# A third load-and-output buffer, an earlier x load and turn, and weight combinations at other places, in a gated scan with a leaky MLP

## Chip, core and metric

One core of a Trainium2 chip runs the whole program. The metric is device time in microseconds (us), from the kernel's start to its end. Engines are named as in the profile: PE multiplies matrices and PEld loads its weights, DVE is the vector engine, ACT the scalar engine, POOL the general one, SP issues most DMAs. A line number such as L203 is a line of the kernel before; in the changed file the same lines stand up to four further on.

## What is computed

```python
sig = 1.0 / (1.0 + np.exp(-f_logit))            # x, f_logit: 4 x 6080 x 256, float32
f = lower_bound + (1.0 - lower_bound) * sig
for t in range(S):
    h = f[:, t] * h + (1.0 - f[:, t]) * x[:, t]
    y[:, t] = h
a = y.reshape(24320, 256) @ w_in                # 256 x 2048
out = np.maximum(0.01 * a, a) @ w_out           # 2048 x 256
```

## The kernel before

The 24320 tokens are cut into 24 blocks, 23 of 1024 tokens and a last one of 768. The hidden width 2048 is cut into eight groups g of 2 x 128 columns. A **slot** is one group of one block, (j, g), and slots run in the order of `seq`. The order of the instructions on every engine is written out by hand: the code is under a manual schedule, and each engine does its list in the order in which the calls stand.

Every float32 operand of a matmul is split into a high and a low part (wi_h and wi_l, yh and yl, gh and gl, the two halves of wo), so a product takes three matmuls. In blocks from 1 on a slot (`slot`, L379) forms the first layer by a scheme with seven products M1 to M7 of block matrices instead of eight, so the stationary weights have seven forms per group: four that are loaded, and three, at places 2 and 4 to 6 of wi_h and wi_l, with combinations of them (`combine_w` adds and subtracts on DVE, `split_c` writes the high parts on ACT and the low parts on DVE). A slot has 21 matmuls for the products and 24 for the second layer (`second`, called at once for the last quarter and through `old` in the next slot for the other three): 45.

Within such a slot PE does M1 into PSUM bank a, M5 into c, M2 into b, M6 into a, the old quarters between M6, M7, M4 and M3, and then one quarter of its own. ACT copies bank a after M1 (L389), after M6 (L396) and after M7 (L401); M6 writes to bank a too, so it waits for the copy at L389. DVE adds bank b (L393), bank c with M5 (L402) and bank c with M3 (L420) to those copies; M5 of the next slot writes bank c, so it waits for L420. For each of the four quarters ACT makes the high part gh (L309) and the full activation (L314), and DVE the low part gl (L319). The last quarter's pair on ACT waits for L420 and stands just ahead of the next slot's L389.

The next block is prepared in the slots of the present one. `hooks` says at which point of which slot: the points of a slot are C (after M1), a0 (after M2), A (after M6), B (ahead of M4), a3 (ahead of M3) and E (the end). In slot 1 the gate's logits are turned (`tl`, two DVE transposes at L203), in slot 2 x is turned (`tx`, the same line), in slots 2 and 3 the gate is formed on ACT (`th` at L206 and `f` at L209), from slot 3 on come u (L212), the scans (L176), differences (L222) and the splits into yh and yl (L227, L230). Block 0 has its own way for all this (`first_slot`, `plain_slot`); its slots form eight products, and between them weights of the later groups are loaded raw, as the two 32-bit halves of each number, decoded on ACT, DVE and POOL (`scale_w`, `decode_w`) and split (`split_w`). Combinations begin in slot 6 of block 0, two slots ahead of block 1's use of group 0, so in block 1 the slots 0 to 5 form those of groups 2 to 7.

The pool `ld` has two buffers of 16 KB per partition. In each block from 1 on they are taken in turn by the output tile of the block before (`new_osb` at C of slot 0), by the logits of the next block (`load` at the same point) and by its x (`load` after the second evacuation in slot 0, L425). All these DMAs stand on SP's queue in that order, with the eight output stores (`evacuate`, L302) between the two loads. `raw` has three buffers of 4 KB of its own in the pool `dw`. `combine_w` puts its result under the tag r, which `scale_w` uses too, with one buffer.

```python
old(s, 1, 1)                                         # L398, after hook("A")
product(a, j, g, M7, False)
act(out=c22[:, :n], in_=a[:, :n], func=ACTF.Copy)    # L401
vtt(out=c22[:, :n], in0=c[:, :n], in1=c22[:, :n], op=ALU.add)   # L402
```

Of the kernel before, what the change touches and what calls it, by code (L numbers as in the profile page):

```python
# [8 lines left out]
F32 = mybir.dt.float32  # L9
F32R = mybir.dt.float32r  # L10
U32 = mybir.dt.uint32
# [13 lines left out]
def tile_gated_scan_then_leaky_mlp(  # L25
# [10 lines left out]
    B, S, D = x.shape  # L36
    NT = B * S
    DFF = w_in.shape[1]
    P = 128
    KC = D // P  # L40
    NG = DFF // P // 2
# [5 lines left out]
    NB = len(starts)  # L47
# [3 lines left out]
    ff = f_logit.rearrange("b s d -> (b s) d")  # L51

    const = ctx.enter_context(tc.tile_pool(name="const", bufs=1))
    ld_p = ctx.enter_context(tc.tile_pool(name="ld", bufs=2))
    xt_p = ctx.enter_context(tc.tile_pool(name="xt", bufs=1))
    cy_p = ctx.enter_context(tc.tile_pool(name="cy", bufs=2))
    ys_p = ctx.enter_context(tc.tile_pool(name="ys", bufs=2))
# [16 lines left out]


    raw_t = {}
    part_t = {}

    def load_w(kind, g):
        r = dw_p.tile([P, 2, 256, 2], U32, tag="raw", name="raw", bufs=3)  # L80
        if kind == "i":
            v = w_in.bitcast(U32).rearrange("(k p) (h g f) -> g h p k f", p=P, h=2, f=2 * P)
            rv = r.rearrange("p h (k f) t -> p h k (f t)", k=2)
            for h in range(2):
                nc.sync.dma_start(out=rv[:, h], in_=v[g, h])
        else:
            v = w_out.bitcast(U32).rearrange("(h g p) f -> g p h f", p=P, h=2)
            nc.sync.dma_start(out=r.rearrange("p h f t -> p h (f t)"), in_=v[g])
        raw_t[kind, g] = r
# [36 lines left out]

    def combine_w(g):
        w = dw_p.tile([P, 4, P], F32, tag="a", name="a")
        c = dw_p.tile([P, 4, P], F32, tag="r", name="r")
        vtt(out=w, in0=wi_h[:, g, 0:4].bitcast(F32), in1=wi_l[:, g, 0:4].bitcast(F32), op=ALU.add)  # L130
        vtt(out=c[:, 0], in0=w[:, 2], in1=w[:, 3], op=ALU.add)
        vtt(out=c[:, 2], in0=w[:, 0], in1=w[:, 2], op=ALU.subtract)
        vtt(out=c[:, 1], in0=c[:, 0], in1=w[:, 0], op=ALU.subtract)
        vtt(out=c[:, 3], in0=w[:, 1], in1=c[:, 1], op=ALU.subtract)
        part_t["c", g] = c
# [61 lines left out]
    def x_piece(j, piece):  # L197
# [35 lines left out]
    hooks = {  # L233
        (1, "A"): [("tl", 0), ("tl", 1)],
        (2, "a0"): [("th", 0)],
        (2, "A"): [("f", 0)],
        (2, "B"): [("tx", 0)],
        (2, "a3"): [("tx", 1)],
        (3, "a0"): [("th", 1)],
        (3, "A"): [("f", 1), ("u", 0), ("scan", (0, 0))],  # L240
        (4, "A"): [("u", 1), ("scan", (0, 1))],
# [137 lines left out]
    def slot(s, hook):  # L379
        j, g = seq[s]  # L380
        n = sizes[j] // 2
        done = g == 0 and j > 0
        a = ps_a.tile([P, HM], F32, tag="a", name="pa")
        b = ps_b.tile([P, HM], F32, tag="b", name="pb")
        c = ps_b.tile([P, HM], F32, tag="c", name="pc")
        product(a, j, g, M1, True)
        hook("C")
        c11 = new_c()
        act(out=c11[:, :n], in_=a[:, :n], func=ACTF.Copy)  # L389
        product(c, j, g, M5, True)  # L390
        product(b, j, g, M2, True)
        hook("a0")
        vtt(out=c11[:, :n], in0=b[:, :n], in1=c11[:, :n], op=ALU.add)  # L393
        product(a, j, g, M6, False)
        c12 = new_c()
        act(out=c12[:, :n], in_=a[:, :n], func=ACTF.Copy)  # L396
        hook("A")
        old(s, 1, 1)  # L398
        product(a, j, g, M7, False)
        c22 = new_c()  # L400
        act(out=c22[:, :n], in_=a[:, :n], func=ACTF.Copy)  # L401
        vtt(out=c22[:, :n], in0=c[:, :n], in1=c22[:, :n], op=ALU.add)  # L402
        leaky_high((j, g, 0, 0), c11)
        leaky((j, g, 0, 0), c11, c11)
        old(s, 1, 0)
        if done:
            evacuate(j - 1, 0)
        low((j, g, 0, 0), c11)
        hook("B")
        leaky_high((j, g, 1, 1), c22)  # L410
        leaky((j, g, 1, 1), c22, c22)
        low((j, g, 1, 1), c22)
        product(a, j, g, M4, False)
        c21 = new_c()
        leaky_high((j, g, 1, 0), a)
        leaky((j, g, 1, 0), c21, a)
        old(s, 0, 1)
        hook("a3")
        product(c, j, g, M3, False)
        vtt(out=c12[:, :n], in0=c[:, :n], in1=c12[:, :n], op=ALU.add)  # L420
        low((j, g, 1, 0), c21)
        if done:
            evacuate(j - 1, 1)
            if j + 1 < NB:
                load(j + 1, "x")  # L425
        leaky_high((j, g, 0, 1), c12)
        leaky((j, g, 0, 1), c12, c12)
        second(j, g, 0, 0)
        low((j, g, 0, 1), c12)
        hook("E")  # L430
# [119 lines left out]
    with tc.manual_schedule():  # L550
# [17 lines left out]
        for s in range(1, len(seq)):  # L568
            j, g = seq[s]

            def hook(at):
# [16 lines left out]
                if j > 0 and (g, at) == (0, "C"):  # L588
                    new_osb(j - 1)
                    if j + 1 < NB:  # L590
                        load(j + 1, "l")
                c = s + 2 - NG
                if 0 <= c < NG:
                    if at == ("D" if j == 0 else "B"):
                        combine_w(c)
                    elif at == "E":
                        split_c(c)
                if j > 0:
                    for p in hooks_own.get((g, at), ()):
                        x_piece(j, p)  # L600
                if j + 1 < NB:
                    for p in hooks.get((g, at), ()):
                        x_piece(j + 1, p)

            (plain_slot if j == 0 else slot)(s, hook)
        e = len(seq)
# [35 lines left out]
```

## Time and profile before

| what | value |
|---|---|
| median of 3 runs | 2017.22 us (2016.95 to 2017.23) |
| the profiled execution, its time | 2017.16 us |
| its span, first to last instruction | 2015.3 us |
| granted TensorE clock, mean | 0.998 |
| busy: PE, PEld, DVE, ACT, POOL | 99%, 81%, 70%, 69%, 1% of the span |
| DMA | 84.6 MB, 42 GB/s on the mean |

A row of the timeline gives when an instruction started and how long it took; in brackets stand the idle time of its engine just ahead of it and what ended that. The next instruction on an engine often starts before the time of the one before it is over, so distances from start to start are compared here: DVE adds of 512 columns last 0.69 us and start 0.60 us apart when nothing holds them. A matmul's time overlaps the next ones in the same way.

### The profile page before, as it was taken

The numbers are of one execution on the slowest core, as the hardware profiler recorded it, in microseconds if no ns is written. First come the engines' busy times: TensorE is split into PE (matmuls) and PEld (weight loads), VectorE is DVE, ScalarE is ACT, GpSimd is POOL, SyncE is SP. The second block draws the span as 40 slices with busy tenths as digits, with TensorE's granted clock in tenths as the row PEclk, the third lists the DMA queues.
The fourth block names the chain that finished last, engine by engine and source line by source line (L and its number), as shares of the span: only waits on it lengthen the run. The fifth ranks groups of instructions, "written<-read, shape, count | busy, mean of one in ns | idle before, by whom it ended". The sixth has DMA issues, their size and how long they took to land.

```text
span 2015.3 us, 23212 instructions
## 1 busy us (share of the span) xinstructions
PE 1988.0 (99%) x8718; PEld 1627.1 (81%) x8718; DVE 1417.0 (70%) x2003; ACT 1399.3 (69%) x2352; POOL 28.0 (1%) x25
## 2 busy tenths in 40 slices
PE   8999999999999999999999999999999999999998
PEld 6777888888888888888888888888888888888888
DVE  7978676767776776767667776676766767676664
ACT  6766667766777667776677667776677666776665
POOL 2200000000000000000000000000000000000000
PEclk9999999999999999999999999999999999999999
DMA  9460522505325054160450514505134052250211
GB/s 187 85 63 1 63 36 28 63 1 63 42 22 63 3 61 50 14 63 10 54 57 7 64 18 46 63 1 63 26 37 63 1 63 35 28 58 0 37 22 16
DMA packets 584448, 84.60 MB, mean 42 GB/s; under 512 B 574096, under 2 KB 582288, under 8 KB 584336
## 3 DMA queue, kind: packets, MB, share of 16 engines
q1 hardware_dynamic: 581184, 82.57, 33.8%
q8 instruction: 68, 1.11, 0.2%
q10 hardware_dynamic: 3152, 0.56, 0.2%
q14 instruction: 44, 0.36, 0.1%
HBM read 58.20 MB, written 24.90 MB: 41 GB/s over the span
## 4 chain that ended last, share of the span: by engine, by line
PE 90%; DVE 6%; ACT 3%; issue 1%; DMA 0%; POOL 0%; DVEq 0%; POOLq 0%; ACTq 0%
PE o L281 48%; PE pa L259 25%; PE pc L259 11%; PE pb L259 6%; DVE xT L203 3%; DVE gl L319 1%; ACT c L314 1%; ACT gh L309 1%; DVE c L420 1%; ACT c L389 1%; DMA lld<-in_f_logit_dram 0%; DVE xT L176 0%; ACT wi_h L140 0%; DVE wi_l L125 0%; DVE osb L296 0%
## 5 line engine op out<-in xcount | busy, mean ns | idle before, releaser
L281 PE MATMUL o<-gh,wo 128*128 128x512 f32 (+1 forms) x3072 | 822.1, 389 | 0.0
L319 DVE TENSOR_TENSOR gl<-c,gh 128x512 fp32r<-128x512 f32 (+1 forms) x768 | 524.4, 686 | 270.5 <-ACT c L314 270.5
L281 PEld LDWEIGHTS o<-gh,wo 128*128 128x128 f32 x3072 | 575.5, 188 | 121.0
L309 ACT ACTIVATE gh<-c 128x512 fp32r<-128x512 f32 (+1 forms) x552 | 342.3, 620 | 193.8 <-DVE c L420 193.8
L281 PE MATMUL o<-gl,wo 128*128 128x512 f32 (+1 forms) x1536 | 472.3, 388 | 0.0
L314 ACT ACTIVATE c<-c 128x512 f32<-128x512 f32 (+1 forms) x552 | 346.5, 628 | 17.6
L281 PEld LDWEIGHTS o<-gl,wo 128*128 128x128 f32 x1536 | 288.0, 188 | 60.6
L259 PE MATMUL pa<-yh,wi_l 128*128 128x512 f32 (+1 forms) x768 | 303.2, 395 | 9.7 <-ACT c L389 5.5
L259 PE MATMUL pa<-yh,wi_h 128*128 128x512 f32 (+1 forms) x768 | 299.1, 389 | 0.9 <-ACT wi_h L123 0.9
L259 PE MATMUL pa<-yl,wi_h 128*128 128x512 f32 (+1 forms) x768 | 298.2, 388 | 0.1
L401 ACT ACTIVATE c<-pa 128x512 f32<-128x512 f32 (+1 forms) x184 | 109.0, 593 | 185.0 <-PE pa L259 182.1
L402 DVE TENSOR_TENSOR c<-pc,c 128x512 f32<-128x512 f32 (+1 forms) x184 | 126.0, 685 | 158.6 <-ACT c L401 154.4
L396 ACT ACTIVATE c<-pa 128x512 f32<-128x512 f32 (+1 forms) x184 | 109.1, 593 | 172.5 <-PE pa L259 169.9
L259 PEld LDWEIGHTS pa<-yh,wi_l 128*128 128x128 f32 x768 | 144.2, 188 | 52.0 <-ACT c L389 17.3
L393 DVE TENSOR_TENSOR c<-pb,c 128x512 f32<-128x512 f32 (+1 forms) x184 | 125.6, 683 | 77.6 <-PE pb L259 64.5
L420 DVE TENSOR_TENSOR c<-pc,c 128x512 f32<-128x512 f32 (+1 forms) x184 | 125.2, 680 | 64.3 <-PE pc L259 63.6
L259 PEld LDWEIGHTS pa<-yl,wi_h 128*128 128x128 f32 x768 | 144.2, 188 | 32.2 <-DVE yl L230 0.8
L259 PEld LDWEIGHTS pa<-yh,wi_h 128*128 128x128 f32 x768 | 144.3, 188 | 29.1 <-ACT wi_h L123 1.1
L259 PE MATMUL pc<-yh,wi_l 128*128 128x512 f32 (+1 forms) x384 | 152.5, 397 | 1.5 <-DVE c L420 1.5
L259 PE MATMUL pc<-yh,wi_h 128*128 128x512 f32 (+1 forms) x384 | 149.7, 390 | 0.0
L259 PE MATMUL pc<-yl,wi_h 128*128 128x512 f32 (+1 forms) x384 | 149.2, 389 | 0.0
L309 ACT ACTIVATE gh<-pa 128x512 fp32r<-128x512 f32 (+1 forms) x200 | 115.3, 576 | 7.0 <-PE pa L259 6.2
(76 smaller groups left out, 1675.9 us busy)
## 6 DMA issues: line engine op xcount, KB each, us to landing
lld<-in_f_logit_dram SPq DMA_DIRECT2D x92, 256.0 KB, 6.5
out_dram<-osb SPq DMA_DIRECT2D x184, 128.0 KB, 3.2
xld<-in_x_dram SPq DMA_DIRECT2D x91, 256.0 KB, 5.8
raw<-in_moe_w_in_dram SPq DMA_DIRECT2D x16, 256.0 KB, 3.5
raw<-in_moe_w_out_dram SPq DMA_DIRECT2D x8, 512.0 KB, 4.4
lld<-in_f_logit_dram SPq DMA_DIRECT2D x4, 192.0 KB, 5.8
xld<-in_x_dram SPq DMA_DIRECT2D x4, 192.0 KB, 5.0
out_dram<-osb SPq DMA_DIRECT2D x5, 96.0 KB, 4.2
```

The lines of the kernel that those rows point to most:

```text
L203: nc.vector.transpose(out=xs[j, nm][:, k], in_=loaded[j, nm][:, k].rearrange("p t d -> p (t d)"))
L259: nc.tensor.matmul(out=bank[:, :n], lhsT=a[:, g, w, :], rhs=b[:, i, :n], start=start and e == 0, stop=stop and e == 2, skip_group_check=True,)
L281: nc.tensor.matmul(out=o[k][:, :n], lhsT=wo[:, g, h, w, k * P:(k + 1) * P], rhs=v[:, :n], start=first and s == 0, stop=last and s == 2, sk ...
L309: act(out=gh[:, :n], in_=src[:, :n], func=ACTF.Prelu, alpha=0.01)
L314: act(out=dst[:, :n], in_=src[:, :n], func=ACTF.Prelu, alpha=0.01)
L319: vtt(out=gl[:, :n], in0=c[:, :n], in1=gh[:, :n].bitcast(F32), op=ALU.subtract)
L389: act(out=c11[:, :n], in_=a[:, :n], func=ACTF.Copy)
L393: vtt(out=c11[:, :n], in0=b[:, :n], in1=c11[:, :n], op=ALU.add)
L396: act(out=c12[:, :n], in_=a[:, :n], func=ACTF.Copy)
L401: act(out=c22[:, :n], in_=a[:, :n], func=ACTF.Copy)
L402: vtt(out=c22[:, :n], in0=c[:, :n], in1=c22[:, :n], op=ALU.add)
L420: vtt(out=c12[:, :n], in0=c[:, :n], in1=c12[:, :n], op=ALU.add)
```

## The change

The pool `ld` gets a third buffer, and its space is found by putting two of the three raw weight buffers of block 0 into a tile of that pool, which is given up afterwards. x of the next block is loaded at C of slot 0, straight after the logits, and turned as a pair at A of slot 2. The combinations of block 1 are formed at C instead of B, into the tag w (two buffers) instead of r; their split stands at A of the next slot, behind the other work of that point, instead of E of the same slot. In block 0 the combinations stay at D and E.

```diff
-    ld_p = ctx.enter_context(tc.tile_pool(name="ld", bufs=2))
+    ld_p = ctx.enter_context(tc.tile_pool(name="ld", bufs=3))
...
     raw_t = {}
+    raws = []
     part_t = {}
 
     def load_w(kind, g):
-        r = dw_p.tile([P, 2, 256, 2], U32, tag="raw", name="raw", bufs=3)
+        if not raws:
+            pair = ld_p.tile([P, 2, 2, 256, 2], U32, tag="ld", name="rawld")
+            raws.extend((dw_p.tile([P, 2, 256, 2], U32, tag="raw", name="raw"), pair[:, 0], pair[:, 1]))
+        r = raws[len(raw_t) % 3]
...
     def combine_w(g):
         w = dw_p.tile([P, 4, P], F32, tag="a", name="a")
-        c = dw_p.tile([P, 4, P], F32, tag="r", name="r")
+        c = dw_p.tile([P, 4, P], F32, tag="w", name="c", bufs=2)
...
-        (2, "A"): [("f", 0)],
-        (2, "B"): [("tx", 0)],
-        (2, "a3"): [("tx", 1)],
+        (2, "A"): [("f", 0), ("tx", 0), ("tx", 1)],
...
             evacuate(j - 1, 1)
-            if j + 1 < NB:
-                load(j + 1, "x")
...
                     if j + 1 < NB:
                         load(j + 1, "l")
+                        load(j + 1, "x")
                 c = s + 2 - NG
-                if 0 <= c < NG:
-                    if at == ("D" if j == 0 else "B"):
-                        combine_w(c)
-                    elif at == "E":
-                        split_c(c)
+                if 0 <= c < NG and at == ("D" if j == 0 else "C"):
+                    combine_w(c)
...
                     for p in hooks.get((g, at), ()):
                         x_piece(j + 1, p)
+                if 0 <= c < NG and j == 0 and at == "E":
+                    split_c(c)
+                elif 0 < c <= NG and at == "A" and ("c", c - 1) in part_t:
+                    split_c(c - 1)
```

Where the instructions stand is shown below at three places, before and after; the line numbers are those of either file, and PE's order is the same in both.

DVE in slot 2 of block 2 (every later block has the same rows): L393, L402 and L420 are the three adds of a slot, L319 the low parts, L203 the turns. Before:

```order
L393 TENSOR_TENSOR c<-pb,c 128x512
L402 TENSOR_TENSOR c<-pc,c 128x512
L319 TENSOR_TENSOR gl<-c,gh 128x512
L203 STREAM_TRANSPOSE xT<-xld 128x1024
L319 TENSOR_TENSOR gl<-c,gh 128x512
L203 STREAM_TRANSPOSE xT<-xld 128x1024
L420 TENSOR_TENSOR c<-pc,c 128x512
L319 TENSOR_TENSOR gl<-c,gh 128x512 x2
```

With the change (L395, L404, L422, L321 and L207 are the same lines, moved):

```order
L395 TENSOR_TENSOR c<-pb,c 128x512
L207 STREAM_TRANSPOSE xT<-xld 128x1024 x2
L404 TENSOR_TENSOR c<-pc,c 128x512
L321 TENSOR_TENSOR gl<-c,gh 128x512 x2
L422 TENSOR_TENSOR c<-pc,c 128x512
L321 TENSOR_TENSOR gl<-c,gh 128x512 x2
```

The two turns went from among the low parts, ahead of the third add, to between the first and the second add.

DVE in block 1, from the second add of slot 3 to the end of that slot. Before:

```order
L402 TENSOR_TENSOR c<-pc,c 128x512
L319 TENSOR_TENSOR gl<-c,gh 128x512
L130 TENSOR_TENSOR a<-wi_h,wi_l 128x512
L131 TENSOR_TENSOR r<-a 128x128
L132 TENSOR_TENSOR r<-a 128x128
L133 TENSOR_TENSOR r<-r,a 128x128
L134 TENSOR_TENSOR r<-a,r 128x128
L319 TENSOR_TENSOR gl<-c,gh 128x512
L420 TENSOR_TENSOR c<-pc,c 128x512
L319 TENSOR_TENSOR gl<-c,gh 128x512 x2
L141 TENSOR_TENSOR wi_l<-r,wi_h 128x128
L141 TENSOR_TENSOR wi_l<-r,wi_h 128x384
```

With the change, from the last low parts of slot 3 to the split in slot 4, which is followed by the second add:

```order
L321 TENSOR_TENSOR gl<-c,gh 128x512 x2
L134 TENSOR_TENSOR a<-wi_h,wi_l 128x512
L135 TENSOR_TENSOR c<-a 128x128
L136 TENSOR_TENSOR c<-a 128x128
L137 TENSOR_TENSOR c<-c,a 128x128
L138 TENSOR_TENSOR c<-a,c 128x128
L395 TENSOR_TENSOR c<-pb,c 128x512
L216 SCALAR_TENSOR_TENSOR xT<-lT,xT 128x1024
L180 SCALAR_TENSOR_TENSOR xT<-lT,xT 128x512
L186 COPY cy<-xT 128x1
L145 TENSOR_TENSOR wi_l<-c,wi_h 128x128
L145 TENSOR_TENSOR wi_l<-c,wi_h 128x384
```

The five instructions of a combination went to ahead of the first add, and the two of the split to ahead of the second; on ACT the split's two instructions went from ahead of L389 to ahead of L401.

SP's queue at the end of block 0 and in block 1. Before:

```order
L85 DMA raw<-in_moe_w_in_dram 128x2x256 x2
L88 DMA raw<-in_moe_w_out_dram 128x2x512
L152 DMA lld<-in_f_logit_dram 32x64x32 x4
L302 DMA out_dram<-osb 64x16x32 x8
L152 DMA xld<-in_x_dram 32x64x32 x4
```

With the change:

```order
L89 DMA rawld<-in_moe_w_in_dram 128x2x256 x2
L92 DMA raw<-in_moe_w_out_dram 128x2x512
L156 DMA lld<-in_f_logit_dram 32x64x32 x4
L156 DMA xld<-in_x_dram 32x64x32 x4
L304 DMA out_dram<-osb 64x16x32 x8
```

The four loads of x now stand ahead of the eight stores of the block before instead of behind them.

## Rows read from the trace of the kernel before

**Rows 1.** The page's part 1: busy us (share of the span) xinstructions.

```profile
PE 1988.0 (99%) x8718; PEld 1627.1 (81%) x8718; DVE 1417.0 (70%) x2003; ACT 1399.3 (69%) x2352; POOL 28.0 (1%) x25
```

**Rows 2.** PE's timeline: start us, us, instruction [idle before <-releaser]; blocks 0, 1, 12, 21.

```profile
52.45 0.50 PE L259 MATMUL pa<-yh,wi_l 128*128 128x512 f32 x1 [0.76 <-DVE wi_l L125]
...
110.82 0.39 PE L259 MATMUL pa<-yh,wi_l 128*128 128x512 f32 x1
...
189.46 0.39 PE L259 MATMUL pa<-yh,wi_l 128*128 128x512 f32 x1
...
1009.16 0.39 PE L259 MATMUL pa<-yh,wi_l 128*128 128x512 f32 x1
...
1019.46 0.39 PE L259 MATMUL pa<-yh,wi_l 128*128 128x512 f32 x1
...
1061.14 0.51 PE L259 MATMUL pa<-yh,wi_l 128*128 128x512 f32 x1 [0.15 <-ACT c L389]
...
1808.13 0.51 PE L259 MATMUL pa<-yh,wi_l 128*128 128x512 f32 x1 [0.15 <-ACT c L389]
```

**Rows 3.** Waits of PE, engine line waited for: us in total, times, longest us.

```profile
PE pa L259 <- ACT c L389: 5.5, 23, 0.8
```

**Rows 4.** ACT's timeline, end of slot 2 of block 12.

```profile
1059.30 0.63 ACT L309 ACTIVATE gh<-c 128x512 fp32r<-128x512 f32 x1 [2.06 <-DVE c L420]
...
1060.51 0.58 ACT L389 ACTIVATE c<-pa 128x512 f32<-128x512 f32 x1
```

**Rows 5.** DVE's timeline, slots 1 and 2 of block 12, slot 1 of block 13 (last row).

```profile
1040.92 2.36 DVE L203 STREAM_TRANSPOSE lT<-lld 128x1024 f32<-128x1024 f32 x2
...
1050.62 0.69 DVE L393 TENSOR_TENSOR c<-pb,c 128x512 f32<-128x512 f32 x1 [0.74 <-PE pb L259]
1053.93 0.69 DVE L402 TENSOR_TENSOR c<-pc,c 128x512 f32<-128x512 f32 x1 [2.63 <-ACT c L401]
...
1058.62 0.65 DVE L420 TENSOR_TENSOR c<-pc,c 128x512 f32<-128x512 f32 x1
...
1060.63 0.69 DVE L319 TENSOR_TENSOR gl<-c,gh 128x512 fp32r<-128x512 f32 x1 [0.77 <-ACT c L314]
...
1122.27 0.65 DVE L319 TENSOR_TENSOR gl<-c,gh 128x512 fp32r<-128x512 f32 x1
```

**Rows 6.** SP's timeline, slot 1 of block 12, and the page's DMA issues (last: us to landing).

```profile
1043.31 5.81 SPq L152 DMA_DIRECT2D xld<-in_x_dram  x4
...
xld<-in_x_dram SPq DMA_DIRECT2D x91, 256.0 KB, 5.8
```

**Rows 7.** DVE's timeline in block 0, slot 2 and then slot 3.

```profile
47.65 0.69 DVE L319 TENSOR_TENSOR gl<-c,gh 128x512 fp32r<-128x512 f32 x1
...
51.71 0.68 DVE L125 TENSOR_TENSOR wi_l<-w,wi_h 128x512 fp32r<-128x512 f32 x1
...
59.68 2.99 DVE L319 TENSOR_TENSOR gl<-c,gh 128x512 fp32r<-128x512 f32 x3
62.60 0.68 DVE L125 TENSOR_TENSOR wi_l<-w,wi_h 128x512 fp32r<-128x512 f32 x1
```

**Rows 8.** DVE's timeline, block 1, end of slot 2 and start of slot 3.

```profile
127.71 0.69 DVE L130 TENSOR_TENSOR a<-wi_h,wi_l 128x512 f32<-128x512 f32 x1
...
129.97 0.68 DVE L420 TENSOR_TENSOR c<-pc,c 128x512 f32<-128x512 f32 x1
...
132.02 0.69 DVE L319 TENSOR_TENSOR gl<-c,gh 128x512 fp32r<-128x512 f32 x1 [0.77 <-ACT c L314]
132.63 0.75 DVE L141 TENSOR_TENSOR wi_l<-r,wi_h 128x128 fp32r<-128x128 f32 x2
133.30 0.68 DVE L393 TENSOR_TENSOR c<-pb,c 128x512 f32<-128x512 f32 x1
```

**Rows 9.** DVE's groups of instructions: shapes xcount | busy us, mean ns | idle before us.

```profile
L176 DVE TENSOR_TENSOR_SCAN xT<-lT,cy,xT 128x512 f32<-128x512 f32 (+1 forms) x46 | 59.2, 1288 | 0.8
...
L212 DVE SCALAR_TENSOR_TENSOR xT<-lT,xT 128x1024 f32<-128x1024 f32 (+1 forms) x46 | 55.3, 1203 | 0.0
```

## Prediction, made before the change was run

> **What bounds the kernel now.** I read first the page's part 1, where PE is busy for 99% of the span [rows 1], then PE's timeline. In the steady part each matmul starts 0.229 us after the one before it: M6 of two neighbouring slots starts at 1009.16 and 1019.46 [rows 2], so a slot without a stall is 10.30 us (45 matmuls), and a block 82.40. The change leaves PE's order alone, so all it can win is time in which PE stands still. M6 of slot 3 starts at 1061.14 in block 12 and at 1808.13 in block 21 [rows 2]: 746.99 us for nine blocks, 83.00 each. So a block loses 0.60 us, and at this place, since the bracket there names the ACT copy L389. PE's list of waits has it 23 times in the run [rows 3]: once a block from block 2 on, and a few more in block 1. What the list books, 5.5 us, is only the idle time; the matmuls beside such a wait also start further apart than 0.229.
>
> How a block comes to that is read backwards in block 12. M6 starts at 1061.14 [rows 2], just after L389, which runs from 1060.51 for 0.58. L389 stands behind the last quarter's gh at 1059.30, which waited 2.06 us for DVE's third add [rows 4]. That add started only at 1058.62 [rows 5], behind the two turns of x and the low parts between them. M6's due time was 1060.66, four slots after 1019.46; slot 2 had begun at 1048.30 (one slot and nine matmuls before that). Inside it DVE had been idle for 2.63 us ahead of its second add at 1053.93, waiting for ACT [rows 5]. So the turns stand in a crowd, with a gap of their own size just ahead.
>
> **The change, part by part.** The sum is made against the profiled execution's 2017.16 us; the median of the runs, 2017.22, is 0.06 above it, and I let one stand for the other. A difference under 0.2% (4 us) is taken as no change.
>
> *x turned at A of slot 2.* The first add starts at 1050.62, and the next DVE instruction can follow 0.60 later, at 1051.22. The pair of the logits' turns, the same operation on the same shape, takes 2.36 [rows 5]. The turns of x then end at 1053.6, and the second add starts at 1053.93 as now: no cost, 0.3 us to spare. What hides them is the wait for ACT; were it shorter, PE would still feel nothing until the second add is 1.5 us late, as worked out below. The low parts and the third add then stand as in slots without turns, and the 0.60 goes. Next in line in slot 3 are ACT's tanh and affine step of the second half; the same pair stands in slot 2, whose M6 is not held. I take the whole of it for blocks 2 to 21: 20 x 0.60 = **12.0 us**. The bounds are 0 and 12.0; nothing else moves in these slots.
>
> *x loaded earlier, third buffer.* Before, x's four loads were issued from 1043.31, in slot 1 of the block that turns it, over 5.81 us [rows 6]: too late for a turn at 1051.22. Now they stand ahead of the stores, and with three takers in three buffers outputs, logits and x each get the same one every time. x's buffer is free once the x before it is turned, in slot 2 of the block before, and SP has nothing ahead of the loads but the logits' loads and older stores. So they are issued there, some 80 us early. The stores behind them wait for nothing new, since the loads are long issued when an evacuation comes. By itself: 0. The third buffer first holds two raw weight buffers; they rotate with the third as three did before, and the last use of that tile, the decoding of group 7's first-layer weights, is over a slot before the first output tile. 0 as well.
>
> *Block 0.* Here too the turns leave the low parts. In slot 2 the first low part starts at 47.65 and the split of group 3's weights at 51.71; in slot 3, where no turn lies between, the same stretch goes from 59.68 to 62.60 [rows 7], 2.92 us. So the split comes at 50.57, 1.14 earlier. PE waited for it at 52.45: 0.76 idle [rows 2] and the 0.16 by which matmuls otherwise overlap (0.39 long, 0.229 apart) make 0.92, and its own 0.50 instead of 0.39 puts the next one 0.11 later. The split now ends at 51.25, ahead of the due time of 51.53. **1.0 us** goes; the bounds are 0 and 1.0. The tag w instead of r spares ACT a wait in slot 7, beside which PE does not wait: 0.
>
> *Block 1, the combinations.* M6 goes from 110.82 in slot 0 to 189.46 in slot 7 [rows 2]: 78.64 against 7 x 10.30 = 72.10, so 6.5 us are lost there, slot 3's turns among them. Part of it is the split at E, two ACT instructions right ahead of L389; part the combination ahead of the third add. Both leave these places. On ACT the split now stands ahead of L401; M4, which follows that copy, comes nine matmuls (2.06 us) after M7, so I take 0. But DVE, from the last low part on, now has combination, first add, the work of point A, split and second add in one row, and I follow that row around. From the third add at 129.97 to the last low part at 132.02 is 2.05 (the add, then ACT's pair L309, L314). From there to the split 0.61, and over the split 0.67, to 133.30. The combination and one low part take 2.26, from 127.71 to 129.97 [rows 8]. The first add takes 0.60. From the second add to the low part that follows it, again an add and ACT's pair, I take the same 2.05. That makes 8.24, plus the work at A: 2.3 for a pair of turns [rows 5]; for u and a scan 1.20 and 1.29 [rows 9], 2.56 with the steps between; 2.75 for two scans with theirs. So the loop takes 10.54 in slot 1, 10.56 in slot 2, 10.8 in slots 3 and 4 and 11.0 in slot 5, against PE's 10.30. M6 starts 0.50 after the last low part (1061.14 after 1060.63 [rows 2, 5]) and is due 2.06 after its slot's start, so it is held once that low part starts over 1.56 after it. An evacuation leaves it at 1.26 (1122.27 [rows 5] in a slot that starts at 1121.01), and it goes to 1.50 (no stall), 1.76 (0.2), 2.06 (0.5), 2.06 (0.5) and 2.26 (0.7), set back each time by PE's own stall; slot 6 has no combination, and there DVE catches up. PE still loses 1.9: **4.6 us** go. The bounds are 0 (the present loss stays) and 6.5.
>
> Sum: 12.0 + 1.0 + 4.6 = 17.6, and 2017.16 - 17.6 = **1999.6 us**.
>
> **Rivals.** *x is not there yet (slower).* If x's buffer still ties its load to slot 1, the pair of turns waits at the head of DVE's queue, ahead of the second add. M6 follows that add by 2.05 + 0.60 + 2.05 + 0.50 = 5.20; with M6 due at 1060.66 the add must start by 1055.46, the pair by 1053.14. Loads issued from 1043.31 have left SP by 1049.12 and land some 5.8 later [rows 6], at the latest at 1054.9. Then the second add comes at 1057.2, 1.76 late, and each of 20 blocks loses 1.16 more than now: 23.2 - 5.6 = 18 slower, 2035. It decides from a pair at 1054.2 on: 1.08 lost in a block, 9.6 more than now in all against the 5.6 won elsewhere, 4 us slower. For it: before, x was not loaded sooner. Against it: SP's new order, and three buffers for the three tiles of a block.
>
> *The 0.60 belongs to slot 3's work on ACT.* The tanh there follows L389. If it held PE, and not the turns, only 5.6 go: 2011.6. Against it, slot 2 has the same pair and no stall, and gh's wait of 2.06 for the third add stands ahead of L389 [rows 4].
>
> *Block 1's loop is longer.* I let instructions overlap: the split's 0.75 ends at 133.38, the next starts at 133.30 [rows 8]. If some seven such steps in a loop each waited for the end of the one before, a loop would take 0.56 more; over slots 2 to 5 that is 2.2, and 0.3 in slot 1: 2.1 us go there instead of 4.6, 2002.1. With the bound, nothing won there, it is 2004.2. The Trainium skill has such a rule: its page "VectorE: DVE Perf Modes", section "The DRAIN you can't avoid", lets the next operation start only when the pipeline is empty, and by it the time would be this rival's. The rows above go against it here.
>
> **How the numbers follow.** The forecast gets 0.80: its main term shows in place and size in equal blocks, and the gap that takes the turns is larger than they are. Block 1's longer loop gets 0.11, ACT's share 0.05, the late x 0.04, of which 0.03 lies past the point of 4 us. Faster by over 0.2% are the forecast, the longer loop and most of the ACT rival: 0.95. Within 0.2%: 0.02. Slower: 0.03. The forecast's own bounds are 1997.7 (block 1 loses nothing) and 2001.5 (its loop starts later). With the longer loop up to its bound the range is 1997.5 to 2004.3; left out are the two other rivals, 0.09, and the forecast's edges.
>
> **What would show it.** Right: M6 of slot 3 82.40 apart from block to block and without a bracket; the two turns of x side by side behind the first add, the second add still waiting for ACT; x's loads right behind the logits', a block ahead of their turn; no wait of PE at the start of slot 3 of block 0; some 74.0 us between M6 of slots 0 and 7 of block 1, with M6 held in slots 3 to 6 by L389. Wrong: a wait of DVE for x's DMA ahead of a turn; M6 of slot 3 still held in every block; a stall in slot 2 that was not there; block 1 near 78.6 again.

## The result and the profile after

| | before | changed |
|---|---|---|
| median of the runs, us | 2017.22 (2016.95 to 2019.25) | 1999.93 (1999.37 to 2001.01) |
| ratio of the times | | 0.9912, 95% interval 0.99 to 0.9923 |
| the profiled execution: time, span | 2017.16, 2015.3 | 2001.01, 1999.2 |

The forecast was 1999.6. In the profiled execution PE stands still for 17.7 us of the span instead of 27.3 (2015.3 less the 1988.0 of [rows 1]); part 1 of the page of the changed kernel:

```profile
PE 1981.5 (99%) x8718; PEld 1633.2 (82%) x8718; DVE 1424.7 (71%) x2003; ACT 1402.6 (70%) x2352; POOL 28.1 (1%) x25
```

The count of instructions is the same on every engine. Line numbers in rows are those of each run's own file: L389, the copy after M1, is L391 in the changed kernel. Where the time went is read on PE, whose order is the same. Its timeline in the changed kernel: the start of slot 3 of block 0 (at 52.45 before), now without a wait, then the start of slot 7 of block 0, M6 of slots 0 and 3 to 7 of block 1, M6 of slot 3 of blocks 12 and 13:

```profile
53.35 0.39 PE L261 MATMUL pa<-yh,wi_l 128*128 128x512 f32 x1
...
98.43 0.50 PE L261 MATMUL pa<-yh,wi_l 128*128 128x512 f32 x1 [0.97 <-DVE wi_l L129]
...
111.59 0.39 PE L261 MATMUL pa<-yh,wi_l 128*128 128x512 f32 x1
...
142.55 0.50 PE L261 MATMUL pa<-yh,wi_l 128*128 128x512 f32 x1
...
153.23 0.50 PE L261 MATMUL pa<-yh,wi_l 128*128 128x512 f32 x1
...
163.99 0.50 PE L261 MATMUL pa<-yh,wi_l 128*128 128x512 f32 x1
...
174.93 0.51 PE L261 MATMUL pa<-yh,wi_l 128*128 128x512 f32 x1
...
185.37 0.39 PE L261 MATMUL pa<-yh,wi_l 128*128 128x512 f32 x1
...
1050.57 0.39 PE L261 MATMUL pa<-yh,wi_l 128*128 128x512 f32 x1
...
1132.96 0.39 PE L261 MATMUL pa<-yh,wi_l 128*128 128x512 f32 x1
```

From slot 3 of block 12 to that of block 13 are 82.39, against 83.00 in [rows 2]: a block of 360 matmuls at 0.2289 and nothing else. In block 1 from M6 of slot 0 to M6 of slot 7 are 73.78 instead of 78.64; a matmul that takes 0.50 instead of 0.39 there was held a little. The wait at 98.43 is the only idle time of PE in brackets after the first 33 us; it stands in the kernel before too (0.96 there, at 97.64).

DVE's timeline of the changed kernel, slot 2 of block 12, answers to [rows 5]:

```profile
1040.52 0.69 DVE L395 TENSOR_TENSOR c<-pb,c 128x512 f32<-128x512 f32 x1 [0.74 <-PE pb L261]
1041.13 2.36 DVE L207 STREAM_TRANSPOSE xT<-xld 128x1024 f32<-128x1024 f32 x2
1043.84 0.69 DVE L404 TENSOR_TENSOR c<-pc,c 128x512 f32<-128x512 f32 x1 [0.35 <-ACT c L403]
```

The pair of turns has gone into the wait of 2.63, of which 0.35 is left. SP's timeline of the changed kernel, the loads of the block that is turned there, and of the next x:

```profile
950.82 5.74 SPq L156 DMA_DIRECT2D lld<-in_f_logit_dram  x4
961.12 5.50 SPq L156 DMA_DIRECT2D xld<-in_x_dram  x4
...
1043.52 5.42 SPq L156 DMA_DIRECT2D xld<-in_x_dram  x4
```

x is issued at 961.12, as soon as the turn of the x before it (another such pair, from 958.73 for 2.36) has freed the buffer, and 80.0 us ahead of its own turn at 1041.13.

**Lost time by stretch.** The start times of PE's 8718 matmuls are in the trace, so the time between two of them, less 0.2289 for each matmul between, is what that stretch lost. Block 0 is taken from its matmul 121 (the ones before make the start-up), block 1 has matmuls 421 to 780, the twenty equal blocks 2 to 21 those up to 7980. All kernels of this study, worked out in this way from their profiled executions, in us:

| kernel | median (lowest to highest) | start of matmul 121 | block 0 | block 1 | 20 blocks |
|---|---|---|---|---|---|
| before | 2017.22 | 37.79 | 2.29 | 6.54 | 11.92 |
| changed | 1999.93 (1999.37 to 2001.01) | 39.62 | 1.24 | 1.67 | -0.08 |
| e1_combos_only | 2012.97 (2012.63 to 2014.57) | 38.17 | 2.29 | 2.30 | 12.03 |
| e2_x_only | 2002.0 (2001.6 to 2003.36) | 37.53 | 1.27 | 4.30 | -0.08 |
| e3_old_turns | 2013.02 (2012.72 to 2015.07) | 37.84 | 2.28 | 2.27 | 11.91 |
| e4_late_load | 2016.12 (2013.71 to 2019.9) | 39.84 | 1.25 | 4.54 | 13.76 |
| e8_one_more_turn | 2000.54 (2000.3 to 2002.6) | 37.58 | 1.27 | 2.98 | -0.08 |
| e9_two_more_turns | 2017.19 (2016.7 to 2017.37) | 37.68 | 2.10 | 4.64 | 14.26 |
| e5_split_low_at_b | 1997.38 (1997.28 to 1998.18) | 37.75 | 1.24 | 0.00 | -0.08 |
| e6_first_combo_later | 1999.79 (1999.2 to 2001.36) | 37.94 | 0.00 | 3.19 | -0.08 |
| e7_both | 1998.77 (1997.86 to 2000.24) | 39.60 | 0.00 | 1.56 | -0.08 |
| e10_one_slot_later | 1997.17 (1996.69 to 1997.62) | 38.72 | 0.02 | 0.32 | -0.08 |
| e11_split_low_at_b_again | 1998.51 (1997.15 to 1999.46) | 39.77 | 1.24 | 0.00 | -0.08 |
| e12_change_again | 1999.15 (1999.05 to 1999.64) | 37.69 | 1.24 | 1.66 | -0.08 |

From before to changed the three stretches win 1.05 + 4.87 + 12.00 = 17.92. The span fell by 16.1 only, since the profiled execution of the changed kernel came to matmul 121 later, by 1.83. That is the start-up, which the change does not touch. The windows view of the changed kernel, 22 to 26 and 26 to 32 us (busy time of PE, PEld, DVE, ACT and POOL, then the granted clock, DMA share and GB/s):

```profile
22.00:26.00 4.00, 3.35 (x8) 2.68 (x9) 3.70 (x5) 2.11 (x4) 1.69 (x2) 0.50 1.39 178
26.00:32.00 6.00, 5.24 (x12) 3.60 (x12) 5.68 (x9) 4.81 (x9) 1.43 (x1) 0.50 1.48 165
```

The same stretches of the same kernel in another execution, e12_change_again:

```profile
22.00:26.00 4.00, 3.43 (x8) 2.75 (x9) 3.69 (x5) 2.07 (x5) 1.76 (x2) 0.50 1.21 210
26.00:32.00 6.00, 5.24 (x21) 3.72 (x21) 5.68 (x9) 4.83 (x10) 1.43 (x2) 0.87 1.52 141
```

In the first one PE stays at 0.50 (1.2 GHz) all the way, and gets 12 matmuls done between 26 and 32; in the second it is back at 2.4 GHz for most of that time, and gets 21 done. Matmul 121 starts at 39.62 in the one and at 37.69 in the other, and the span is 1999.2 and 1997.3. Of the 14 profiled executions nine start matmul 121 between 37.5 and 38.2, four between 39.6 and 39.9 and one at 38.72, whatever the kernel. In the four late ones the granted clock is back at 1.00 only at 32 us, in the other ten by 28. So differences under 2 us are read from the table of losses and not from single times.

### The profile page after: what moved, and what is told of

The parts are those of the page before. It is cut to its first block, busy times and chain, and to the rows that moved or that the text cites. A ratio compares the mean times of both kernels' runs of the same rounds, so it can differ in the third digit from the quotient of the medians.

```text
span 1999.2 us, 23268 instructions
## 1 busy us (share of the span) xinstructions
PE 1981.5 (99%) x8718; PEld 1633.2 (82%) x8718; DVE 1424.7 (71%) x2003; ACT 1402.6 (70%) x2352; POOL 28.1 (1%) x25
## 4 chain that ended last, share of the span: by engine, by line
PE 95%; DVE 3%; ACT 1%; issue 0%; DMA 0%; POOL 0%; ACTq 0%; DVEq 0%; POOLq 0%
PE o L283 50%; PE pa L261 25%; PE pc L261 13%; PE pb L261 6%; DVE gl L321 1%; DVE xT L180 0%; ACT c L316 0%; ACT gh L311 0%; DMA lb<-in_lower_bound_dram 0%; DVE c L422 0%; DVE osb L298 0%; DVE c L404 0%; DVE a L134 0%; DVE lT L226 0%; DVE wi_l L129 0%
## 5 line engine op out<-in xcount | busy, mean ns | idle before, releaser
L321 DVE TENSOR_TENSOR gl<-c,gh 128x512 fp32r<-128x512 f32 (+1 forms) x768 | 526.8, 689 | 282.2 <-ACT c L316 282.2
L261 PE MATMUL pa<-yh,wi_l 128*128 128x512 f32 (+1 forms) x768 | 297.9, 388 | 2.3 <-DVE wi_l L129 2.1
L404 DVE TENSOR_TENSOR c<-pc,c 128x512 f32<-128x512 f32 (+1 forms) x184 | 126.2, 686 | 99.8 <-ACT c L403 95.5
L395 DVE TENSOR_TENSOR c<-pb,c 128x512 f32<-128x512 f32 (+1 forms) x184 | 126.0, 685 | 92.6 <-PE pb L261 79.8
L422 DVE TENSOR_TENSOR c<-pc,c 128x512 f32<-128x512 f32 (+1 forms) x184 | 126.0, 685 | 73.7 <-PE pc L261 73.1
```

What stands on the lines that cost most here:

```text
L261: nc.tensor.matmul(out=bank[:, :n], lhsT=a[:, g, w, :], rhs=b[:, i, :n], start=start and e == 0, stop=stop and e == 2, skip_group_check=True,)
L321: vtt(out=gl[:, :n], in0=c[:, :n], in1=gh[:, :n].bitcast(F32), op=ALU.subtract)
```

## The experiments

**The two halves of the change, and the turns put back.** e1 is the kernel before with the combinations as in the change:

```diff
-        c = dw_p.tile([P, 4, P], F32, tag="r", name="r")
+        c = dw_p.tile([P, 4, P], F32, tag="w", name="c", bufs=2)
...
-                if 0 <= c < NG:
-                    if at == ("D" if j == 0 else "B"):
-                        combine_w(c)
-                    elif at == "E":
-                        split_c(c)
+                if 0 <= c < NG and at == ("D" if j == 0 else "C"):
+                    combine_w(c)
...
+                if 0 <= c < NG and j == 0 and at == "E":
+                    split_c(c)
+                elif 0 < c <= NG and at == "A" and ("c", c - 1) in part_t:
+                    split_c(c - 1)
```

> The kernel before, with only the combinations of the weights moved as in the change (the result in tag w, made at C, split a slot later at A). x is turned at B and a3 and loaded late, as before. If the sum of the prediction adds up term by term: block 1 loses about 2 us instead of 6.5, less the 0.6 that the turns of x still take in its slot 3, so about 4.3 us go and the time is about 2012.9; the wait at the start of slot 3 of block 0 and the 0.60 in each of 20 blocks stay. Rival, block 1's gain needs the turns gone as well: nearly nothing goes, 2016 to 2017. Rival, the combinations' new place is what empties slot 3 in every block: near 2000.

e2 is the changed kernel with the same lines turned round (- for +).

> The changed kernel, with the combinations at their old places (tag r, made at B, split at E). If the terms add up: 12.0 in blocks 2 to 21, 1.0 in block 0 and about 0.6 to 2 of block 1 go against the kernel before, so the time is 2001.6 to 2003.6, and the changed kernel is faster than this one by 2 to 4 us, all of it in block 1. Rival, block 1's gain came with the turns' move alone: the same as the changed kernel, 1999.4 to 2000.

e3 is the changed kernel with the turns where they were:

```diff
-        (2, "A"): [("f", 0), ("tx", 0), ("tx", 1)],
+        (2, "A"): [("f", 0)],
+        (2, "B"): [("tx", 0)],
+        (2, "a3"): [("tx", 1)],
```

> The changed kernel, third buffer and early load kept, with the two turns of x put back at B and a3. My theory, the turns' place is what counts and the early load only allows it: M6 of slot 3 is held in every block again, 12.0 us, block 0's wait is back, 1.0, and the time is 2012 to 2013.5, the same as with the combinations alone. Rival, the late load was part of the 0.60 (the turns waited for x, or its loads delayed something): clearly less than 2012, down to 2000 if it was all of it.

Measured: 2012.97, 2002.0 and 2013.02, ratios to before 0.9977 (0.9967 to 0.9986), 0.9923 (0.991 to 0.9935) and 0.998 (0.9971 to 0.9989). All three came out as the sum has it. The 20 blocks lose 12 us in e1 and e3 and nothing in e2 and in the changed kernel: with the load early in both (e3 and the changed kernel), this goes by the place of the turns. With the third buffer and the early load kept (e3), M6 of slot 3 is held exactly as in [rows 2]; PE's timeline of e3:

```profile
1056.89 0.51 PE L263 MATMUL pa<-yh,wi_l 128*128 128x512 f32 x1 [0.15 <-ACT c L393]
```

ACT's work in slot 3 is the same in e2 and e3, so the rival that gave it the 0.60 is out. In block 1 the combinations alone win 6.54 - 2.30 = 4.24, the turns alone 6.54 - 4.30 = 2.24, both together 4.87. Nearly all of the overlap lies in one stretch, from M6 of slot 2 to M6 of slot 3: it loses 2.86 in the kernel before, 0.67 in e1, 0.61 in e2 and 0.06 in the changed kernel. There combination and turns both stood ahead of the same third add, and what one has taken away the other can't take again. So the rival of e2, that the turns brought all of block 1's gain, is out too, and simple adding of the two would have overrated them by 1.61.

**The load that comes late.** e4 is e1 with the turns at A of slot 2 and nothing else: two buffers, x loaded in slot 1.

```diff
-        (2, "A"): [("f", 0)],
-        (2, "B"): [("tx", 0)],
-        (2, "a3"): [("tx", 1)],
+        (2, "A"): [("f", 0), ("tx", 0), ("tx", 1)],
```

> The turns of x at A of slot 2 and the combinations as in the change, but two buffers and the load of x late, in slot 1 as before. It tests the rival by which x is not there yet. By that mechanism the pair of turns waits at the head of DVE's queue for x: with the landing some 5.6 us after the slot's start, as the loads landed in the kernel before, the pair starts 3 us after the first add, the second add 0.8 to 1.0 late beyond its margin of 1.5, and each of 20 blocks loses 0.75 to 1.0: 2014 to 2019; with the latest landing that the prediction allowed, about 2030. If the load's time does not matter, the time is that of the change, about 2000.

Measured: 2016.12, ratio 0.9994 (0.9985 to 1.0003), all of the change's gain in the blocks gone. DVE's timeline of e4, slot 2 of block 12 and of block 13:

```profile
1050.02 0.69 DVE L391 TENSOR_TENSOR c<-pb,c 128x512 f32<-128x512 f32 x1 [0.74 <-PE pb L257]
...
1053.51 2.37 DVE L203 STREAM_TRANSPOSE xT<-xld 128x1024 f32<-128x1024 f32 x2 [2.80 <-DMA xld<-in_x_dram]
1055.80 0.65 DVE L400 TENSOR_TENSOR c<-pc,c 128x512 f32<-128x512 f32 x1
...
1133.45 0.69 DVE L391 TENSOR_TENSOR c<-pb,c 128x512 f32<-128x512 f32 x1 [0.74 <-PE pb L257]
1137.55 2.37 DVE L203 STREAM_TRANSPOSE xT<-xld 128x1024 f32<-128x1024 f32 x2 [3.40 <-DMA xld<-in_x_dram]
1139.84 0.65 DVE L400 TENSOR_TENSOR c<-pc,c 128x512 f32<-128x512 f32 x1
```

The turns stand at the head of DVE's queue and wait for x, which lands at another moment in each block; so each of the 20 blocks loses between 0.0 and 1.63 (0.69 on the mean), and this kernel's runs scatter over 6 us. The slower rival's mechanism is real, then, and the early load with its third buffer is what keeps the change from it, though by itself (e3) it wins nothing. Whether two buffers would do for an early load was not tried. PE's timeline of e4 in block 12:

```profile
1056.51 0.50 PE L257 MATMUL pc<-yh,wi_l 128*128 128x512 f32 x1 [0.40 <-DVE c L400]
...
1060.98 0.50 PE L257 MATMUL pa<-yh,wi_l 128*128 128x512 f32 x1
```

The late second add (L400) is felt first by M3, which writes the bank that it reads, and only then by M6 of the next slot. The prediction followed the path to M6 alone.

**How late the second add may come.** The changed kernel, with the turn of x's second half issued twice (e8, whose edit is shown) or three times (e9):

```diff
-        (2, "A"): [("f", 0), ("tx", 0), ("tx", 1)],
+        (2, "A"): [("f", 0), ("tx", 0), ("tx", 1), ("tx", 1)],
```

> The changed kernel with the turn of x's second half done three times instead of once at A of slot 2, so 2.4 us more VectorE work there. The prediction said that PE feels nothing until the second add is 1.5 us late, and that the gap there was 0.3. By that the second add comes about 2.1 late, 0.4 to 0.6 us beyond the margin, and each of 20 blocks loses that: 8 to 12 us slower than the changed kernel, with M6 of a slot held in each block. Rival, the gap ahead of the second add was slack only in appearance and any delay of it is paid at once: about 2.1 in each block, 42 us slower. Rival, VectorE has far more room than 1.5: no difference.

> The changed kernel with the turn of x's second half done twice at A of slot 2. The turn takes 1.23 and the second add has 0.35 of idle time ahead of it, so it comes 0.9 late. If the margin of 1.5 us holds, blocks 2 to 21 and block 0 lose nothing, and block 1, where VectorE's loop already holds PE, loses some 1.2: 2000.5 to 2001 against 1999.4 to 1999.9. Rival, the margin is smaller than it reads and each block pays what goes beyond the idle time: 18 us slower, 2018; with half that margin 3 us more in all.

Measured: e9 2017.19, 17 us slower than the changed kernel, where 8 to 12 were expected; e8 2000.54, as expected. DVE's timeline in slot 2 of block 12, e9:

```profile
1049.39 0.69 DVE L395 TENSOR_TENSOR c<-pb,c 128x512 f32<-128x512 f32 x1 [0.74 <-PE pb L261]
1050.00 4.92 DVE L207 STREAM_TRANSPOSE xT<-xld 128x1024 f32<-128x1024 f32 x4
1054.84 0.65 DVE L404 TENSOR_TENSOR c<-pc,c 128x512 f32<-128x512 f32 x1
```

And e8:

```profile
1039.81 0.69 DVE L395 TENSOR_TENSOR c<-pb,c 128x512 f32<-128x512 f32 x1 [0.74 <-PE pb L261]
1040.42 3.64 DVE L207 STREAM_TRANSPOSE xT<-xld 128x1024 f32<-128x1024 f32 x3
1043.98 0.65 DVE L404 TENSOR_TENSOR c<-pc,c 128x512 f32<-128x512 f32 x1
```

In the changed kernel the second add starts 3.32 after the first (1043.84 after 1040.52). With the rows of e4 that makes four pairs of lateness and loss in one block:

| kernel, block | second add after the first | later by | the block loses |
|---|---|---|---|
| e8, 12 | 4.17 | 0.85 | 0.0 |
| e9, 12 | 5.45 | 2.13 | 0.71 |
| e4, 12 | 5.78 | 2.46 | 1.03 |
| e4, 13 | 6.39 | 3.07 | 1.63 |

Where there is a loss, it is 1.42, 1.43 and 1.44 below the lateness: that is the margin, where the prediction had read 1.5. The 14.3 of the 20 blocks in e9 are thus 0.7 a block, where 0.4 to 0.6 was expected; what the expectation left out are block 1 (2.97 more than in the changed kernel, 4.64 - 1.67) and block 0 (0.86). In block 1 DVE's loop has no room for the 2.56 of two more turns (4.92 - 2.36). But the 2.97 are not the price of that work alone, since PE's clock falls there. PE's timeline of e9 in block 1:

```profile
139.55 0.63 PE L261 MATMUL pc<-yh,wi_l 128*128 128x512 f32 x1 [2.07 <-DVE c L404]
...
143.30 0.40 PE L261 MATMUL pa<-yh,wi_l 128*128 128x512 f32 x1
```

The windows view of e9, 140 to 143 us:

```profile
140.00:143.00 3.00, 3.00 (x9) 2.35 (x8) 1.98 (x4) 2.55 (x6) 0.00 (x0) 0.50 1.30 170
```

After the wait of 2.07 PE works at a granted clock of 0.50 (1.2 GHz). From 139.55 to 143.30 are nine matmuls in 3.75, where nine at 0.2289 take 2.06: 1.69 more. PE is then so late that DVE does not hold M6 in the next slots, as it does in the changed kernel. In e4 the same happens at the same place (a wait of 2.12, then 0.50), so its 4.54 in block 1 have a part of this too. In no other of these executions does the clock fall between the start-up and the last microseconds. e8, where it stays up, shows block 1 by itself: 1.31 more there for one turn, and next to nothing elsewhere. Neither of e8's rivals holds.

**What block 1 and block 0 still lose.** The changed kernel's loop in block 1, DVE's timeline: the last low parts of slots 0 to 5, and between two of them, slot 2 in full but for the four small adds of the combination:

```profile
121.10 0.65 DVE L321 TENSOR_TENSOR gl<-c,gh 128x512 fp32r<-128x512 f32 x1
...
131.55 0.69 DVE L321 TENSOR_TENSOR gl<-c,gh 128x512 fp32r<-128x512 f32 x1 [0.77 <-ACT c L316]
132.16 0.68 DVE L134 TENSOR_TENSOR a<-wi_h,wi_l 128x512 f32<-128x512 f32 x1
...
133.82 0.68 DVE L395 TENSOR_TENSOR c<-pb,c 128x512 f32<-128x512 f32 x1
134.42 2.36 DVE L207 STREAM_TRANSPOSE xT<-xld 128x1024 f32<-128x1024 f32 x2
136.70 0.72 DVE L145 TENSOR_TENSOR wi_l<-c,wi_h 128x128 fp32r<-128x128 f32 x2
137.34 0.69 DVE L404 TENSOR_TENSOR c<-pc,c 128x512 f32<-128x512 f32 x1
137.94 0.68 DVE L321 TENSOR_TENSOR gl<-c,gh 128x512 fp32r<-128x512 f32 x1
139.39 0.69 DVE L321 TENSOR_TENSOR gl<-c,gh 128x512 fp32r<-128x512 f32 x1 [0.77 <-ACT c L316]
...
142.05 0.69 DVE L321 TENSOR_TENSOR gl<-c,gh 128x512 fp32r<-128x512 f32 x1 [0.77 <-ACT c L316]
...
152.72 0.69 DVE L321 TENSOR_TENSOR gl<-c,gh 128x512 fp32r<-128x512 f32 x1 [0.76 <-ACT c L316]
...
163.49 0.69 DVE L321 TENSOR_TENSOR gl<-c,gh 128x512 fp32r<-128x512 f32 x1 [0.77 <-ACT c L316]
...
174.43 0.70 DVE L321 TENSOR_TENSOR gl<-c,gh 128x512 fp32r<-128x512 f32 x1 [0.77 <-ACT c L316]
```

The loops take 10.45, 10.50, 10.67, 10.77 and 10.94, against PE's 10.30. Twice in each DVE waits 0.77 for ACT. e5 puts the split's DVE half, 0.72 long, behind the second add and the first low part, so that it stands in such a wait:

```diff
-    def split_c(g):
+    def split_c(g, part="hl"):
...
-                elif 0 < c <= NG and at == "A" and ("c", c - 1) in part_t:
-                    split_c(c - 1)
+                elif j > 0 and 0 < c <= NG and at in "AB" and ("c", c - 1) in part_t:
+                    split_c(c - 1, "h" if at == "A" else "l")
```

> The changed kernel; in block 1 the VectorE half of the split of a combination goes from A (ahead of the second add) to B (behind it), where VectorE waits 0.77 us for ACT ahead of the next low part. Theory, VectorE's loop of 10.5 to 10.94 us is what holds M6 there: the loop falls by some 0.6 to 0.7, to about PE's 10.30, the 1.68 us that block 1 still loses go almost wholly, and the time falls by 1.2 to 1.7 us against the changed kernel. Rival, ACT's or another engine's loop holds M6: no difference.

Measured: 1997.38, with block 1 at 0.00. DVE's timeline of e5, slot 2 of block 1:

```profile
129.14 0.69 DVE L323 TENSOR_TENSOR gl<-c,gh 128x512 fp32r<-128x512 f32 x1 [0.77 <-ACT c L318]
...
135.25 0.69 DVE L323 TENSOR_TENSOR gl<-c,gh 128x512 fp32r<-128x512 f32 x1 [0.30 <-ACT c L318]
135.86 0.75 DVE L147 TENSOR_TENSOR wi_l<-c,wi_h 128x128 fp32r<-128x128 f32 x2
...
139.44 0.69 DVE L323 TENSOR_TENSOR gl<-c,gh 128x512 fp32r<-128x512 f32 x1 [0.77 <-ACT c L318]
```

From 129.14 to 139.44 are 10.30: the loop is now PE's. So DVE's row of work was what held M6 in block 1, as the prediction had it.

e6 goes after the wait at 98.43, where the first combination stands ahead of the split of group 7's weights; e7 has the edits of e5 and e6. The edit of e6:

```diff
-                if 0 <= c < NG and at == ("D" if j == 0 else "C"):
+                if 0 <= c < NG and at == ("E" if c == 0 else "D" if j == 0 else "C"):
                     combine_w(c)
...
-                if 0 <= c < NG and j == 0 and at == "E":
+                if c == 1 and at == "W":
+                    split_c(0)
+                if c == 1 and at == "E":
                     split_c(c)
-                elif 0 < c <= NG and at == "A" and ("c", c - 1) in part_t:
+                elif 0 < c <= NG and j > 0 and at == "A" and ("c", c - 1) in part_t:
```

> The changed kernel; the first combination, of group 0 in the last slots of block 0, is made at E of slot 6 instead of D, behind the split of group 7's weights, and split at W of the next slot. Theory: the wait of PE for the split of group 7's weights at the start of slot 7 (about 1.1 us idle and 0.1 of a longer matmul) goes, and the time falls by about 1.2 us. Rival, the combination only moves in front of another thing that PE waits for: no difference, or a new wait in slots 6 and 7.

> The changed kernel with both edits, the VectorE half of block 1's splits at B and the first combination later. If both theories hold, the gains add: 2.4 to 2.9 us less than the changed kernel, about 1997, with no stall left between block 0's slot 3 and the last block.

Measured: 1999.79 and 1998.77; both theories missed. The wait at 98.43 is gone (block 0 loses nothing), but block 1 loses 1.52 more than in the changed kernel. PE's timeline of e6, slot 0 of block 1:

```profile
109.00 0.50 PE L261 MATMUL pa<-yh,wi_l 128*128 128x512 f32 x1 [0.18 <-ACT c L391]
...
112.62 0.50 PE L261 MATMUL pa<-yl,wi_h 128*128 128x512 f32 x1 [0.82 <-DVE yl L234]
```

From the split of group 7's weights (at 94.34 in e6) to the first add of block 1 (112.49) DVE has four splits and three combinations besides its other work, and what is put back in one slot is late in the next. So the work itself has to leave them. e10 forms every combination a slot later; the split comes in that same slot, from block 1 on in the two halves of e5:

```diff
-                c = s + 2 - NG
+                c = s + 1 - NG
...
-                if 0 <= c < NG and j == 0 and at == "E":
+                if c == 0 and at == "E":
                     split_c(c)
-                elif 0 < c <= NG and at == "A" and ("c", c - 1) in part_t:
-                    split_c(c - 1)
+                elif 0 < c < NG and at in "AB":
+                    split_c(c, "h" if at == "A" else "l")
```

> The changed kernel with the whole chain of combinations one slot later (the first in the last slot of block 0, none in the slot where group 7's weights are split), and in block 1 the split in the same slot as its combination, its ScalarE half at A and its VectorE half at B. Making the first combination merely later inside its slot moved 1.24 us from block 0 into 1.52 us at the start of block 1, so the work has to leave the slot, not only its place in it. Theory: the wait for group 7's split goes (1.24) and block 1 loses nothing, as with the split at B alone: 2.9 us less lost than in the changed kernel, 1.2 less than with the split at B, around 1996.2. Rival: the combination one slot later holds the first slots of block 1, and the time is that of the split at B alone, 1997.4, or above.

> The kernel with VectorE's half of the split at B once more, beside the changed kernel and the one with the chain a slot later on one chip. It lost 1.67 us less than the changed kernel between slot 1 and the end; executions of one kernel lie up to 2 us apart by the start-up stretch at the lower clock. Theory: 1997.3 to 1999.3, with the median 1.0 to 2.5 below the changed kernel's.

> The changed kernel itself, beside the two kernels that are to beat it. Theory: 1999.2 to 2001.0, two clusters some 1.8 us apart by the length of the start-up stretch at the lower granted clock; M6 and all later matmuls of blocks 2 to 21 without a stall in either.

Measured on one chip: 1997.17 (1996.69 to 1997.62), 1998.51 (1997.15 to 1999.46) and 1999.15 (1999.05 to 1999.64). e10 loses 0.34 us in blocks 0 and 1, 2.57 less than the changed kernel, where 2.9 were expected. What is left is one wait of M5 in the first slot of block 1 for the split of the first combination (L147), which the load of its weights shows; PEld's and PE's timeline of e10:

```profile
108.31 0.19 PEld L263 LDWEIGHTS pc<-yh,wi_l 128*128 128x128 f32 x1 [0.48 <-DVE wi_l L147]
108.31 0.50 PE L263 MATMUL pc<-yh,wi_l 128*128 128x512 f32 x1
```

The matmul starts 0.44 after the one before it instead of 0.23, and the next one 0.34 after it. e10 beats both kernels, ratio to before 0.9897 (0.9882 to 0.9912); its runs all lie below all of the changed kernel's. e11, the same kernel as e5, came out only 0.64 below the changed kernel's median, where 1.0 or more was expected: in its profiled execution matmul 121 started at 39.77, in the changed kernel's at 37.69, and the table has the 1.66 all the same. Of the two groups that were expected of the changed kernel one came. Between e10 and e5 the times alone can't tell, since the start-up's spread is larger than the 0.90 between their losses.

## Why the prediction was right

- **Blocks 2 to 21, 12.0.** Right in mechanism and size: 11.92 lost before, nothing after (-0.08 by the rounding of the step), and e3 brings it back by the turns' place alone. The pair was to end 0.3 ahead of the second add; 0.35 of wait is left.
- **The margin.** The prediction read 1.5 us of delay that PE would not feel; the measured blocks give 1.43. It went by M6 alone, and M3 is held as well, ahead of it; the two together lose within 0.1 us of what the path to M6 gave.
- **The early load, 0.** Right: e3 against e1, 2013.02 and 2012.97. It was predicted some 80 us early, and is. The rival "x is not there yet" got 0.04; e4 shows that with two buffers and the load at its old place it would have come, with 0.69 lost in a block on the mean where the latest landing gave 1.76, and 2016 where that gave 2035.
- **Block 0, 1.0.** 1.05, and the wait is gone from the start of slot 3.
- **Block 1, 4.6.** 4.87. The loops were put at 10.54, 10.56, 10.8, 10.8 and 11.0, and take 10.45, 10.50, 10.67, 10.77 and 10.94: each a little shorter, so 1.67 is lost where 1.9 was predicted. 73.78 between the two M6 stand against "some 74.0". M6 is held in slots 3 to 6, as was said; a part of it falls on M3, which was not.
- **The longer loop.** That rival is out, since the loops are shorter than the forecast's and not longer. The row at 132.16 above starts 0.61 after the one at 131.55 that lasts 0.69, so the next operation does start before the one before has ended. The rule of the Trainium skill's page "VectorE: DVE Perf Modes", section "The DRAIN you can't avoid", read as a wait for the end of every operation, does not hold for these neighbours; the section itself adds that an operation that is not held starts earlier, which the rival left out.
- **What the sum did not have.** The terms come to 17.6 and measured 17.92; the profiled executions differ by 16.15, as the start-up of the changed one was 1.83 longer. The prediction took one execution's time as if the start-up were constant. The runs of the changed kernel lie on both sides of the forecast for this reason (1999.05 to 2001.01 in two sets), and part of the closeness of 1999.6 and 1999.93 is luck: with the shorter start-up the median was 1999.15.

## What to carry to other kernels

Work that is off the critical engine still has a right place: look on its queue for a wait that is as long as the work, move the work into it, and check that its data are there by then, for at the head of a queue a late load holds everything behind it. The slack behind such a place is measured cheaply, by issuing the work twice: here one extra turn cost the steady blocks nothing and two cost 0.70 each. Read it in stretches that stay at one clock: in block 1 two extra turns made PE wait 2.07, and its clock fell as well. Two edits that empty the same stretch don't add up, and a piece of work that is put later within a full stretch only moves its wait; it has to leave the stretch.

## What was not expected of the hardware

After a wait of 2.6 us (2.0 in e10) PE works at a granted clock of 0.50 near the start of each of these executions, and how long it stays there differs from one execution of the same kernel to the next: in the two shown it was back at 1.00 only at about 32 us in one and by 28 us in the other, with the same waits of 2.6 and 0.76 ahead of it. That moves the whole program by some 2 us, more than the 1.67 that e5 wins. What makes the difference between two executions was not settled.

In the middle of the program, in block 1 of e9 and of e4, a single wait of PE of 2.07 and of 2.12 was followed by the lower clock too, and in e9 that cost nine matmuls 1.69 us.

The landing of one load of 1 MB varied from block to block enough to move DVE's turn by over a microsecond: 49.9 us of waits of DVE for x in e4 make 2.4 on the mean of 21 waits, the longest 3.4. The first add comes 7.3 after the loads' first issue in nearly every block, the turn between 9.4 and 11.4 after it, and the block's loss goes from 0.0 to 1.63 with that.
